# ReLU-squared attention and a SwiGLU block on one core: the second half's norm on VectorE, head groups of four and early second-half scores in batch 0, and stream slots that begin another group

## The chip, the cores and the metric

The kernel runs on one core of a Trainium2 chip. The metric is device time in microseconds of that core. The kernel before took 448.42 us (median of 3 runs, 448.09 to 448.57). The profile is one further execution of the same program; it took 447.78 us, of which the instructions span 446.0 us.

A core has a matrix engine (TensorE, PE in the profile; PEld is its weight loads), VectorE (DVE), ScalarE (ACT), GpSimd (POOL, which here issues nearly all loads) and SyncE (SP, which here issues DMA transposes and the stores). Each engine runs its own instructions in the order in which the program lists them, and waits on semaphores for the others.

## The reference

```python
# q, k, v: (8, 12, 448, 64) float32;  S = 448, D = 64
scores = matmul(q, k.T) / sqrt(D)
attn   = maximum(scores, 0)**2 / S
x      = matmul(attn, v)                 # heads side by side: (3584, 768)

rms = sqrt(mean(x*x, axis=-1) + 1e-6)
xn  = x / rms * rms_g
g   = xn @ w_gate                        # 768 x 1536
val = xn @ w_val                         # 768 x 1536
out = (g * sigmoid(g) * val) @ w_out     # 1536 x 768
```

There is no softmax, so the scores need only a ReLU and a square. The norm needs the sum of squares over all twelve heads of a token; nothing of the feed-forward part of a batch can begin before that batch's attention is complete.

## The kernel before

**Tiling.** There are eight batches of 448 tokens. Scores are made transposed (keys on partitions, queries along the row), two heads of a pair at a time, into a pair of PSUM banks; a rectangle r of 128 x 896 is made by a ReLU (ScalarE, line 459, or VectorE, line 457) and squared in place by VectorE (line 462). `attend` (line 597) multiplies four heads' rectangles with v, ScalarE writes the result as xT (line 632). `rest` (line 511) makes the scores of the last 64 keys of two head pairs. Rectangles live in a ring of 14 SBUF tiles, `r_ring`; a rectangle can be made only when the `attend` that read its tile last is over.

Batch 0 alone is cut into two halves of 224 queries (`halves`, `attention_half(0)` and `attention_half(HS)`, scores on line 493), so that the feed-forward part can begin when half of the queries have been attended. Its q and k are loaded in three pieces of heads (0-2, 2-6, 6-12) and turned on TensorE (`transposes`, lines 412 and 420; VectorE copies the result out, line 430). For each half of batch 0 `Sums` (line 857) adds up the squares over the heads with a matrix of ones, and `norm_scale` makes 1/rms on ScalarE as Exp(-0.5 Ln(mean + eps)) (lines 675 and 679). This needs the Ln/Exp table, and Silu needs another: a table load (line 383) stands on either side. Six VectorE instructions (line 684) then make xn.

**The stream.** The feed-forward part (line 809) is a stream of groups. A group accumulates one output tile in one PSUM bank: a gate or value projection over 6 blocks of 128 contraction rows, or an output projection over 12. Each block is split into its upper and lower 64 rows (half 0 and half 1), which run in different halves of the array. A slot of the stream (`Stream.step`) takes one matmul of half 0 from one group (the lead) and one of half 1 from another (the follow), so that both halves of the array work; where `pick` finds no lead or no follow the slot holds one half only. A group enters with half 0 and ends with half 1. In the quarter form each of these is cut again into two of 64 columns. Silu (line 880), the product with the value (hT, line 894) and the copies of the output (line 954) empty the banks.

**What sets the order.** The whole program is listed by a planner that runs when the kernel is built. Every piece of work is an `Op` with a cost for each engine that can do it, the ops that it needs, a rank and sometimes a due time; `Planner.run` lets time pass by these costs, gives each engine the ready op of the lowest rank, and lists the instructions in that order. The costs are not times of the chip: they decide order alone. A change of a rank or of a dependency therefore moves instructions in the whole program. Where the planner sees TensorE idle for over 0.3 us in the early part, `fill` lists matmuls of zeros (line 1071) that nobody reads.

**Queues.** POOL issues the loads in the order of the `load` calls, each waiting until the eighth load before it has landed (`pool_dma`). They are q, k and v of batch 0, the eight slices of the gate and value weights, q, k, v of batch 1, the output weights, and then the later batches. k of batch 0 is staged in the tile of the output weights, wo_sb.

Of the kernel before, what the change touches and what calls it, by code (L numbers as in the profile page):

```python
# [9 lines left out]
BF16 = mybir.dt.bfloat16  # L10
ALU = mybir.AluOpType
# [8 lines left out]
class Op:  # L20


    def __init__(self, on, fn, deps=(), rank=0, pair=None, bank=False, ends=None, due=None, ring=None,
                 early=0.0, lean=(), form=None):
        self.on, self.ring, self.early = on, ring, early
        self.fn, self.deps, self.rank = fn, list(deps), rank
        self.pair, self.bank, self.ends, self.due = pair, bank, ends, due
        self.done = self.left = NEVER
        self.lean, self.form = dict(lean), form
        self.ps = None  # L30
# [15 lines left out]
class Ring:  # L46


    def __init__(self, tiles):
        self.tiles, self.users, self.at = tiles, [[] for _ in tiles], 0  # L50

    def ready(self):
        return max((u.done for u in self.users[self.at]), default=0.0)
# [1 line left out]
    def take(self, users):  # L55
        n = self.at
        self.before = self.users[n]
        self.users[n], self.at = list(users), (n + 1) % len(self.tiles)
        return self.tiles[n]


class Planner:
# [105 lines left out]
def kernel(  # L168
# [52 lines left out]
    def tiles(n, shape, dtype, name):  # L221
        return [work.tile(shape, dtype, name=f"{name}{i}", tag=f"{name}{i}") for i in range(n)]

    r_ring = Ring(tiles(14, [P, 2, S], BF16, "r"))
    sil_ring = Ring(tiles(3, [P, S], BF16, "sil"))
    ost_ring = Ring(tiles(3, [P, DM], FP32, "ost"))
    xT_of = tiles(2, [P, KT, S], BF16, "xT")
    xn_of = tiles(2, [P, KT, S], BF16, "xn")
    acc_of = tiles(2, [P, 2, S], FP32, "acc")
    x2 = tiles(1, [P, 2, S], FP32, "x2")[0]  # L230
    sum_of = tiles(2, [P, S], BF16, "ssum")
    rstd_of = tiles(2, [P, S], FP32, "rstd")
    hT = tiles(1, [P, FT, 2 * S], BF16, "hT")[0]
# [213 lines left out]

    def evict_rect(t, n, key, group):

        r = r_ring.take([Later(avs, group)])  # L450
        rects[key] = r

        def relu(op):
            op.view = r[:, :, : n // 2]
            src = t.ps.tile[:, :, : n // 2]
            if op.engine == "DVE":
                nc.vector.tensor_relu(out=op.view, in_=src)  # L457
            else:
                nc.scalar.activation(out=op.view, in_=src, func=ACT.Relu)  # L459

        def square(op):
            nc.vector.tensor_tensor(out=rl.view, in0=rl.view, in1=rl.view, op=ALU.mult)  # L462

        rl = add(Op({"ACT": 0.05 + n * 0.833e-3, "DVE": 0.07 + n * 1.042e-3}, relu,
                    [t] + r_ring.before, rank=2, lean={"DVE": 0.5 if key[:2] == (0, 0) else 1.5 if key[0] == 0 else 0.9}))
        sq = add(Op({"DVE": 0.06 + n * 0.53e-3}, square, [rl], rank=3))
        return rl, sq

    def scores_full(b, j, c, due):
# [57 lines left out]
    def rest(b, j, lo, w, due):  # L527
        def fn(op):
            emit_rest(op.ps.tile, b, j, lo, w)
            rl, sq = evict_rect(op, 2 * w, (b, lo, j, "rest"), (b, lo, j))  # L530
            rests[b, lo, j] = (sq, rl)
            plan.take(op.ps.banks, [rl])

        need = [Turned(b, j), Turned(b, j + 1)] + ([Issued(ones[b, lo, j - 2])] if j else [])
        return add(Op({"PE": 0.0025 + w / 2400.0}, fn, need, rank=-4 if j else -1,
                      pair=wide, due=due, form="q", ring=r_ring, early=0.4))

    class Turned(Op):
# [127 lines left out]

    xns, xn_ops = {}, {}

    def norm_scale(b, lo, w, g):

        rstd = accs[b, lo][2]

        def root(op):
            act_set(LN_EXP)
            nc.scalar.activation(
                out=rstd[:, :w], in_=g.ps[:, :w], func=ACT.Ln, scale=1.0 / float(DM),
                bias=eps_col[:],
            )
            nc.scalar.activation(out=rstd[:, :w], in_=rstd[:, :w], func=ACT.Exp, scale=-0.5)  # L679

        def scale(kt):
            def fn(op):
                xns[b] = xn_of[b % 2]
                nc.vector.scalar_tensor_tensor(  # L684
                    out=xns[b][:, kt, lo : lo + w], in0=xTs[b][:, kt, lo : lo + w],
                    scalar=g_sb[:, kt : kt + 1], in1=rstd[:, :w], op0=ALU.mult, op1=ALU.mult,
                )
            return fn

        rt = add(Op({"ACT": lambda: 2 * (0.22 + w * 0.833e-3) + switch(LN_EXP)}, root, [g.end],  # L690
                    rank=-1))
        plan.take(g.space.banks, [rt])
        xn_ops[b, lo] = [
            add(Op({"DVE": 0.126 + w * 1.05e-3}, scale(kt), [rt], rank=-1)) for kt in range(KT)
        ]
        add(Op({"ACT": lambda: switch(SILU)}, lambda op: act_set(SILU), [rt], rank=6))

    def ready_for_norm(b):
        need = [Later(sil, (b, FT - 1, lo)) for lo, _ in halves(b)]
# [3 lines left out]
    class Stream:  # L703
# [38 lines left out]

        def step(self, t):
            lead = self.pick(0, None, t)
            if lead is not None and lead not in self.open:
                self.todo.remove(lead)
                self.open.append(lead)
                lead.begin()
            follow = self.pick(1, lead, t)
            pair = [(half, g) for half, g in ((0, lead), (1, follow)) if g is not None]  # L750
            assert pair
            state["quarters"] = any(g.quarters for _, g in pair) or any(
                g.quarters and g.count[0] for g in self.open
            )
            for m in blocks():
                for half, g in pair:
                    g.emit(half, *m)
            for half, g in pair:
                g.emitted(half, t)
            self.at = [lead, follow]  # L760
            self.steps += 1
            took = max(g.slot for _, g in pair) + plan.changed(form())
            if follow is not None and follow.count[1] == follow.n:
                self.open.remove(follow)
                follow.finish(t)
            note = pair[0][1].note
            if note is not None:
                state["phase"] = note
            return took
# [248 lines left out]
    def now():  # L1018
        return True

    def attention_half(lo):
        for j in range(0, HP, 2):
            if lo == 0:
                transposes(0, j)
                transposes(0, j + 1)
            for jj in range(2):
                scores_half(0, lo, [(j + jj, 0), (j + jj, 1)], now)
            scores_half(0, lo, [(j, 2), (j + 1, 2)], now)
            if j == 0:
                rest(0, 0, lo, HS, now)  # L1030
            attend(0, j, lo, HS, now)
            if j + 2 < HP:
                rest(0, j + 2, lo, HS, now)

    def attention_full(b):
# [38 lines left out]

    load("q", 0, 0, 2)
    load("k", 0, 0, 2)
    load("q", 0, 2, 6)
    load("k", 0, 2, 6)
    made["ident"] = add(Op({"POOL": 0.6}, lambda op: masks.make_identity(nc, ident[:])))
    load("q", 0, 6, 12)  # L1080
    load("k", 0, 6, 12)
    load("v", 0, 0, 6)
    load("v", 0, 6, 12)
    for s in range(NSL):
# [5 lines left out]
    load_wo(0, 2)  # L1090
    load_wo(1, 2)

    attention_half(0)
    first = Sums(0, [(0,), (2,), (4,)])
    for b in range(B):
        groups = ffn(b)
        if b == 0:
# [66 lines left out]
```

## Time and profile before

| what | value |
|---|---|
| median of 3 runs | 448.42 us (448.09 to 448.57) |
| the profiled execution: its time, its span | 447.78 us, 446.0 us |
| PE busy | 440.7 us (99%), 7846 matmuls |
| of these, matmuls of zeros | 110, busy 14.5 us |
| ACT, DVE, POOL busy | 268.2, 240.2, 76.6 us |
| ACT table loads | 18, 23.1 us |
| first slot of the stream begins | 27.24 us |
| first slot with batch 0's second half | 50.4 us |

Busy time of PE counts every matmul, those of zeros as well, and an overlap of matmuls once. "x" is a number of instructions. The chain is the work that ended last, followed backwards, so each of its pieces held up the next.

### The profile page before, as it was taken

How to read it: one execution, taken by the hardware profiler on the slowest of the kernel's cores; microseconds unless marked ns; L12 is line 12 of the kernel's file. 1: busy time of each engine (PE TensorE's matmuls, PEld its weight loads, DVE VectorE, ACT ScalarE, POOL GpSimd, SP SyncE). 2: the span in 40 equal slices, each digit the busy share in tenths (PEclk: the TensorE clock that was granted, in tenths of full speed). 3: DMA queues.
4: the chain of work that ended last, by engine and by line, in shares of the span. 5: the costliest groups of instructions: out<-in, count | busy, mean ns of one | idle time of the engine just before them, and what ended most of it. 6: DMA issues, size and time to landing. Idle time of an engine off the chain costs nothing.

```text
span 446.0 us, 17081 instructions
## 1 busy us (share of the span) xinstructions
PE 440.7 (99%) x7846; PEld 328.6 (74%) x7846; DVE 240.2 (54%) x401; ACT 268.2 (60%) x395; POOL 76.6 (17%) x96
## 2 busy tenths in 40 slices
PE   8999999999999999999999999999999999999996
PEld 7678776877868777678779765678778755687785
DVE  1975786475645455466656347466655446432210
ACT  1677696586648665586757666587657666342212
POOL 8522710070080070070000350010000000000000
PEclk9999999999999999999999999999999999999999
DMA  9999999899899799599005899880002200030004
GB/s 109 196 204 201 202 188 86 137 186 112 99 135 126 139 188 103 107 175 125 1 4 96 153 177 54 114 161 20 3 1 69 75 5 3 1 93 17 3 10 134
DMA packets 130359, 44.75 MB, mean 100 GB/s; under 512 B 102256, under 2 KB 126832, under 8 KB 130288
## 3 DMA queue, kind: packets, MB, share of 16 engines
q0 software_dynamic: 90912, 24.39, 58.5%
q1 hardware_dynamic: 38992, 18.94, 21.3%
q8 instruction: 61, 1.00, 0.9%
q10 hardware_dynamic: 384, 0.34, 0.3%
q14 instruction: 10, 0.08, 0.1%
HBM read 48.76 MB, written 11.01 MB: 134 GB/s over the span
## 4 chain that ended last, share of the span: by engine, by line
PE 97%; DVE 1%; ACT 0%; issue 0%
PE psP L809 78%; PE psS L597 7%; PE psS L475 6%; PE psP L1071 3%; PE psS L511 1%; PE psP L420 1%; PE psS L493 1%; DVE r L462 1%; PE psP L857 0%; PE psP L412 0%; DVE qkT L430 0%; DVE r L457 0%; ACT r L459 0%; DVE xn L636 0%; ACT ost L954 0%
## 5 line engine op out<-in xcount | busy, mean ns | idle before, releaser
L809 PE MATMUL psP<-xn,wg_sb 64*64 64x448 bf16 (+1 forms) x2304 | 219.5, 339 | 0.1
L809 PE MATMUL psP<-xn,wv_sb 64*64 64x448 bf16 (+1 forms) x2304 | 202.8, 339 | 0.2
L459 ACT ACTIVATE r<-psS 128x896 bf16<-128x896 f32 (+1 forms) x168 | 147.7, 913 | 47.8 <-PE psS L475 23.1
L809 PEld LDWEIGHTS <-wg_sb 64*64 64x64 bf16 (+1 forms) x2304 | 122.2, 105 | 36.1 <-PE psP L809 8.0
L462 DVE TENSOR_TENSOR r<-r 128x896 bf16<-128x896 bf16 (+1 forms) x171 | 102.4, 614 | 72.7 <-ACT r L459 72.0
L809 PE MATMUL psP<-wo_sb,hT 64*128 64x384 bf16 (+2 forms) x1526 | 139.4, 321 | 0.0
L809 PEld LDWEIGHTS <-wv_sb 64*64 64x64 bf16 (+1 forms) x2304 | 117.0, 105 | 29.3 <-issue 4.4
L809 PEld LDWEIGHTS <-hT 64*128 64x128 bf16 (+1 forms) x1526 | 102.3, 96 | 22.4 <-issue 2.4
L894 DVE TENSOR_TENSOR hT<-sil,psP 128x448 bf16<-128x448 bf16 (+1 forms) x108 | 60.9, 566 | 64.2 <-PE psP L809 49.9
L880 ACT ACTIVATE sil<-psP 128x448 bf16<-128x448 f32 (+1 forms) x108 | 54.6, 507 | 64.7 <-PE psP L809 55.1
L954 ACT COPY ost<-psP 128x384 f32<-128x384 f32 (+1 forms) x56 | 26.5, 474 | 44.0 <-PE psP L809 42.7
L475 PE MATMUL psS<-qkT 64*64 64x448 bf16 (+1 forms) x412 | 49.8, 350 | 0.0
L597 PE MATMUL psS<-r,vb 64*64 64x448 bf16 (+1 forms) x756 | 46.0, 331 | 0.1
L291 POOL DMA_DIRECT2D vb<-in_v_dram x20 | 14.2, 722 | 179.4 <-PE psS L475 99.9
L684 DVE SCALAR_TENSOR_TENSOR xn<-xT,g_sb,rstd 128x448 bf16<-128x448 bf16 (+1 forms) x54 | 30.3, 629 | 22.7 <-ACT rstd L679 22.7
L307 POOL DMA_DIRECT2D kb<-in_k_dram x42 | 33.3, 1025 | 17.4 <-DMA wo_sb<-in_moe_w_out_dram 9.4
L597 PEld LDWEIGHTS <-vb 64*64 64x64 bf16 x756 | 24.6, 106 | 9.7 <-issue 1.4
L632 ACT ACTIVATE xT<-psS 128x896 bf16<-128x896 f32 (+1 forms) x27 | 22.5, 833 | 14.2 <-PE psS L597 14.1
L475 PEld LDWEIGHTS <-qkT 64*64 64x64 bf16 (+1 forms) x412 | 21.4, 103 | 6.2 <-issue 0.4
L383 ACT ACT_TABLE_LOAD x18 | 23.1, 1283 | 1.0 <-PEq L1148 0.7
L642 DVE TENSOR_TENSOR x<-xT 128x896 f32<-128x896 bf16 x14 | 15.2, 1089 | 6.7 <-ACT xT L632 6.7
L1071 PE MATMUL psP<-busy_bf,ones_bf 128*128 128x224 bf16 x110 | 14.5, 291 | 1.3 <-DVE eps_col L368 1.3
(41 smaller groups left out, 144.1 us busy)
## 6 DMA issues: line engine op xcount, KB each, us to landing
vb<-in_v_dram POOLq DMA_DIRECT2D x12, 384.0 KB, 7.7
qb<-in_q_dram POOLq DMA_DIRECT2D x6, 672.0 KB, 13.8
kb<-in_k_dram POOLq DMA_DIRECT2D x42, 96.0 KB, 12.5
out_dram<-ost SPq DMA_DIRECT2D x7, 336.0 KB, 3.0
wg_sb<-in_moe_w_gate_dram POOLq DMA_DIRECT2D x4, 576.0 KB, 15.9
wv_sb<-in_moe_w_val_dram POOLq DMA_DIRECT2D x4, 576.0 KB, 17.2
wo_sb<-in_moe_w_out_dram POOLq DMA_DIRECT2D x2, 1152.0 KB, 15.1
out_dram<-ost SPq DMA_DIRECT2D x8, 288.0 KB, 4.5
```

The source lines that it names most:

```text
L307: behind_of[b] = nc.gpsimd.dma_start(out=to[:, u - u0 : u - u0 + step, h0:h1, :], in_=rows[:, u : u + step])
L383: nc.scalar.add_instruction(mybir.InstLoadActFuncSet(name=name, act_func_set_id=n, ins=[], outs=[]))
L459: nc.scalar.activation(out=op.view, in_=src, func=ACT.Relu)
L462: nc.vector.tensor_tensor(out=rl.view, in0=rl.view, in1=rl.view, op=ALU.mult)
L475: nc.tensor.matmul(out=ps[m0:m1, hh, :S], lhsT=qkT[b][prt, j, 0, c * P + m0 : c * P + m1], rhs=qkT[b][prt, j, 1, :], start=True, stop=True,)
L597: mm = nc.tensor.matmul(out=ps[hh * D : (hh + 1) * D, jj, :w], lhsT=vb[prt, 2 * (j + jj) + hh, u * D : (u + 1) * D], rhs=r[prt, hh, :], st ...
L684: nc.vector.scalar_tensor_tensor(out=xns[b][:, kt, lo : lo + w], in0=xTs[b][:, kt, lo : lo + w], scalar=g_sb[:, kt : kt + 1], in1=rstd[:, ...
L809: mm = nc.tensor.matmul(out=self.ps[m0:m1, : self.w], lhsT=self.lhsT(i)[prt, m0:m1], rhs=self.rhs(i)[prt], start=(half == 0 and i == 0), s ...
L880: nc.scalar.activation(out=s[:, :w], in_=g.ps[:, :w], func=ACT.Silu)
L894: nc.vector.tensor_tensor(out=hT[:, fb, o : o + w], in0=sil[b, fb, lo][1][:, :w], in1=g.ps[:, :w], op=ALU.mult,)
L954: nc.scalar.copy(out=to, in_=g.ps[:, :w])
L1071: nc.tensor.matmul(out=s.tile[:, :HS], lhsT=ones_bf[:], rhs=busy_bf[:, :HS], start=True, stop=True)
```

## The change

There are four parts.

1. **Loads and order of batch 0.** q and k come in four groups of heads (0-2, 2-4, 4-8, 8-12) in place of three, which makes eight loads of them in place of six. The scores of the second half for the first four head pairs are offered beside those of the first half (`half_scores(HS, j, early)`, which prefers them while the planner's time is under 13), and the `rest` of a head pair no longer waits for the `attend` before it. Evictions of these early scores have a later rank (`aside`). `Sums` of the first half is created ahead of the attention.
2. **More places for rectangles.** Six more tiles, each used once, are views of x2 and of the two acc tiles, which batch 0 does not otherwise use before its norm.
3. **The second half's norm.** `inverse_root` makes 1/rms of batch 0's second half with eleven VectorE instructions of 128 x 224 (a first guess by an integer shift, then two refining steps), in place of Ln and Exp on ScalarE with their two table loads. Their scratch space is x2.
4. **Stream.** Where a slot of batches 1 to 6 has a lead but no follow, and another group could begin, that other group becomes the lead and the first one may serve a later slot.

```diff
 class Ring:
-    def __init__(self, tiles):
-        self.tiles, self.users, self.at = tiles, [[] for _ in tiles], 0
+    def __init__(self, tiles, once=()):
+        self.tiles, self.keep = list(tiles) + list(once), len(tiles)
+        self.users, self.at = [[] for _ in self.tiles], 0
...
-        return self.tiles[n]
+        tile = self.tiles[n]
+        if self.at == 0:
+            del self.tiles[self.keep :]
+        return tile
...
-    r_ring = Ring(tiles(14, [P, 2, S], BF16, "r"))
...
+    spare = []
+    for t in (x2, *acc_of):
+        flat = t.bitcast(BF16)
+        spare += [flat[:, i, :].rearrange("p (t s) -> p t s", t=2) for i in range(2)]
+    r_ring = Ring(tiles(14, [P, 2, S], BF16, "r"), spare)
...
     def evict_rect(t, n, key, group):
+        aside = key[:2] == (0, HS) and not first.end.done < NEVER
...
-                    [t] + r_ring.before, rank=2, lean={"DVE": 0.5 if key[:2] == (0, 0) else 1.5 if key[0] == 0 else 0.9}))
-        sq = add(Op({"DVE": 0.06 + n * 0.53e-3}, square, [rl], rank=3))
+                    [t] + r_ring.before, rank=4 if aside else 2, lean={"DVE": 0.5 if key[:2] == (0, 0) else 1.5 if key[0] == 0 else 0.9}))
+        sq = add(Op({"DVE": 0.06 + n * 0.53e-3}, square, [rl], rank=5 if aside else 3))
...
-        need = [Turned(b, j), Turned(b, j + 1)] + ([Issued(ones[b, lo, j - 2])] if j else [])
+        need = [Turned(b, j), Turned(b, j + 1)] + ([Issued(ones[b, lo, j - 2])] if j and (b or lo) else [])
...
+    def inverse_root(g, y, w):
+        x, h, t = (x2[:, i // 2, i % 2 * HS : i % 2 * HS + w] for i in range(3))
+        as_int = lambda v: v.bitcast(mybir.dt.int32)
+        ts, tt, stt = nc.vector.tensor_scalar, nc.vector.tensor_tensor, nc.vector.scalar_tensor_tensor
+        steps = [
+            lambda: ts(out=x, in0=g.ps[:, :w], scalar1=1.0 / float(DM), scalar2=eps, op0=ALU.mult, op1=ALU.add),
+            lambda: ts(out=as_int(h), in0=as_int(x), scalar1=1, scalar2=None, op0=ALU.logical_shift_right),
+            lambda: ts(out=as_int(y), in0=as_int(h), scalar1=-1.0, scalar2=float(0x5F3759DF), op0=ALU.mult, op1=ALU.add),
+            lambda: tt(out=h, in0=y, in1=y, op=ALU.mult),
+            lambda: tt(out=h, in0=h, in1=x, op=ALU.mult),
+            lambda: ts(out=t, in0=h, scalar1=0.375, scalar2=-1.25, op0=ALU.mult, op1=ALU.add),
...
+            lambda: stt(out=y, in0=t, scalar=1.5, in1=y, op0=ALU.add, op1=ALU.mult),
+        ]
...
-        rt = add(Op({"ACT": lambda: 2 * (0.22 + w * 0.833e-3) + switch(LN_EXP)}, root, [g.end],
-                    rank=-1))
-        plan.take(g.space.banks, [rt])
+        if (b, lo) == (0, HS):
+            rt = inverse_root(g, rstd[:, :w], w)
+        else:
+            rt = add(Op({"ACT": lambda: 2 * (0.22 + w * 0.833e-3) + switch(LN_EXP)}, root, [g.end],
+                        rank=-1))
+            plan.take(g.space.banks, [rt])
...
-        add(Op({"ACT": lambda: switch(SILU)}, lambda op: act_set(SILU), [rt], rank=6))
+        add(Op({"ACT": lambda: switch(SILU)}, lambda op: act_set(SILU), [rt], rank=6 if b else -1))
...
         def step(self, t):
             lead = self.pick(0, None, t)
+            follow = self.pick(1, lead, t)
+            if lead is not None and follow is None and lead.note and 0 < lead.note[0] < B - 1:
+                for g, r in self.options(0, lead):
+                    if g is not lead and lead.last == 0 and r <= t + self.CLOSE:
+                        lead = g
+                        follow = self.pick(1, g, t)
+                        break
...
+    def early():
+        return plan.now < 13.0
+    EARLY = 4
+    def half_scores(lo, j, due):
+        for jj in range(2):
+            scores_half(0, lo, [(j + jj, 0), (j + jj, 1)], due)
+        scores_half(0, lo, [(j, 2), (j + 1, 2)], due)
+        if j == 0 or not lo:
+            rest(0, j, lo, HS, due)
...
+            if lo == 0 or j >= EARLY:
+                half_scores(lo, j, now)
+            if lo == 0 and j < EARLY:
+                half_scores(HS, j, early)
             attend(0, j, lo, HS, now)
-            if j + 2 < HP:
+            if lo and j + 2 < HP:
                 rest(0, j + 2, lo, HS, now)
...
-    load("q", 0, 2, 6)
-    load("k", 0, 2, 6)
+    load("q", 0, 2, 4)
+    load("k", 0, 2, 4)
...
-    load("q", 0, 6, 12)
-    load("k", 0, 6, 12)
+    for h in (4, 8):
+        load("q", 0, h, h + 4)
+        load("k", 0, h, h + 4)
...
+    first = Sums(0, [(0,), (2,), (4,)])
     attention_half(0)
-    first = Sums(0, [(0,), (2,), (4,)])
```

## The prediction

> **What bounds the kernel now.** I read the page first, then the chain in order of time, then the timeline of ScalarE where the chain looked odd, and last the busy time by stretch.
>
> ```profile
> span 446.0 us, 17081 instructions
> PE 440.7 (99%) x7846; PEld 328.6 (74%) x7846; DVE 240.2 (54%) x401; ACT 268.2 (60%) x395; POOL 76.6 (17%) x96
> ...
> L1071 PE MATMUL psP<-busy_bf,ones_bf 128*128 128x224 bf16 x110 | 14.5, 291 | 1.3 <-DVE eps_col L368 1.3
> ```
>
> TensorE is the bound: it is never idle for long, and no other engine passes 60%. But 99% is no proof that nothing can be gained. 110 matmuls are zeros, and a slot of the stream with one half takes as long as a slot with two. So the question is how much of TensorE's time is empty. The chain shows it (start, length, what):
>
> ```profile
> 1.29 6.56 PE psP L1071 x42
> ...
> 9.60 1.06 PE psP L1071 x10
> ...
> 32.49 0.51 PE psS L597 x16
> 32.99 0.10 PE psS L511 x4
> ...
> 33.29 0.41 PE psS L597 x12
> ...
> 33.91 0.20 PE psS L493 x4
> ...
> 45.84 0.97 PE psP L809 x12
> 46.81 0.05 issue
> 46.86 2.78 PE psP L809 x40
> ```
>
> After the first 42, a matmul of zeros takes 1.06/10 = 0.106 us, and there are 68 of them before the stream begins at 27.24. At 45.84, 12 matmuls of the stream take 0.97 us and the next 40 take 2.78; in pairs at 0.095 us a slot (batch 0's slots of 224 start 0.095 to 0.096 apart) they would take 0.57 and 1.90. What is late there, ScalarE's timeline tells:
>
> ```profile
> 43.55 1.28 ACT L383 ACT_TABLE_LOAD   x1
> 44.84 0.45 ACT L675 ACTIVATE rstd<-psP,eps_col 128x224 f32<-128x224 f32 x1
> 45.32 0.39 ACT L679 ACTIVATE rstd<-rstd 128x224 f32<-128x224 f32 x1
> 45.73 1.28 ACT L383 ACT_TABLE_LOAD   x1
> 47.02 0.61 ACT L880 ACTIVATE sil<-psP 128x224 bf16<-128x224 f32 x2
> ```
>
> From 43.55 to 47.02 no Silu runs, so banks of the stream stay full and it finds no second group to pair. The second half's own first slot begins only at 50.42, when its xn (last one ended at 48.0) had long been there: the norm's harm is the blocked ScalarE.
>
> From 60 us on PE is busy 382.5 of 382.6 us; no engine and no DMA makes it wait. There a gain can come only from fewer slots. A stretch late in the kernel, from the chain:
>
> ```profile
> 387.97 8.06 PE psP L809 x93
> ```
>
> 93 matmuls in pairs at 0.1625 us would be 7.56 us. Six of them stand alone (six starts in a row 0.162 apart, from 391.57): (93+6)/2 = 49.5 slots, 8.04 us. A lone half costs a full slot.
>
> **The change part by part.** The order of the two programs, instruction by instruction, gives the counts; the trace of before gives the prices.
>
> *Head (loads in fours, early scores, 20 places for rectangles).* Ahead of the first slot of the stream stand 110 matmuls of zeros before and 86 after; real work moved ahead of it is 5 scores (0.20 each), 2 rests (0.10) and one attend (0.51 + 0.41): 2.1 us. If the first slot begins when it did, TensorE has 2.1 us less behind it; the 24 zeros fewer are 24 x 0.106 = 2.5 us. I take -2.3, with -2.6 and 0 as ends: 0 where the first slot is late by as much.
>
> Is it late? It needs the first half's Ln, which follows ScalarE's evictions. Before, 7 rectangles of 896, 3 of 448 and 3 xT stand ahead of it; after, 14, 4 and 3. Three of 896 in a row take 2.56 us (0.82 apart), the small ones 0.54: 14 x 0.82 + 4 x 0.54 + 3 x 0.55 = 15.3 us of the 16.15 us between the first ReLU (9.64) and Ln (25.79). It fits with 0.8 us left, where before it had 7. At 0.92 each, as a lone one takes, it is 16.7: 0.5 late. I take +0.2 (0 to +0.5).
>
> *Two more loads.* Each costs POOL 0.62 to 0.79 us of issue, so v and the first weight slices are issued up to 1.4 us later. DMA is the limit there: weight slices land 2.9 us apart (23.61, 26.51, 29.47, ... 41.06) in the order of bytes, and POOL sat idle until a landing before four loads between 21 and 30 (1.59, 2.10, 2.13 and 2.30 us). I take 0; without that cover it is +1.4. The order on SP moves two stores of 0.3 to 0.45 us ahead of a block of transposes; after 60 us nothing waits for a DMA on the chain: 0.
>
> *Form switches.* Changes between whole, half-row, quarter and transpose forms rise from 72 to 77. Weight loads show 0.17 to 0.18 us of idle at such a switch, partly under running matmuls; I take 0.12 each, +0.6 (0 to +0.9).
>
> *Second half's norm.* ScalarE loses two table loads, Ln and Exp (3.4 us). The empty part of the chain at 45.8, (0.97 + 2.78) - (0.57 + 1.90) = 1.3 us, and 0.1 of issue, go: -1.4 (-1.0 where some lone slots remain there).
>
> VectorE gains 11 instructions of 128 x 224 on a chain of dependence. No row shows them; the nearest are line 684 (0.38 each in a row of six) and hT of 224 (0.34), and, far off, 1.09 for an fp32 result of four times the size (line 642). At 0.38 they are 4.2 us, with three hT between them (1.1) and six xn (2.3): 7.6 us from the sum to the last xn. In the new order 92 slots of the first half stand between that sum and the first slot of the second half, 92 x 0.095 = 8.8 us. So the root is covered, with 1.2 us left; at 1.09 it would not be, and 6.6 us would lie open. But one product hT is due every 12 slots (1.15 us), and three root steps with one hT take 1.5: hT runs late and a bank comes free late. +0.3 (0 to +1.0).
>
> The Trainium skill, "VectorE: DVE Perf Modes", Mode 2x_2P, has fp32 steps with one tensor from SBUF at two elements a cycle, and those with two tensors at one: as an estimate three steps of 0.12 and eight of 0.23 us, 2.2 us in all before what each instruction costs to start; by that hT would not be late, and the sum would be 0.3 better. No row of before has such steps.
>
> *Stream.* All slots: 2053 before, 2031 after. By length: 12 fewer of 224 (those are the norm's stretch above), 6 fewer of 448, 4 fewer of 384. Slots of 448 start 0.189 apart: 6 x 0.189 + 4 x 0.1625 = -1.8. Some lone slots next to scores already cost only 0.045 to 0.06, so the other end is -1.2. More slots now pair two output pieces in the quarter form (21 against 2). Around the one at 247.64, thirteen starts in a row take 2.37 us, no more than at 0.189 each, so that is free.
>
> Sum: -2.3 + 0.2 + 0.6 - 1.4 + 0.3 - 1.8 = -4.4 us. The profiled execution took 447.78 us (span 446.0 and 1.8 around it): 443.4. The median shown is 0.64 above that execution, so on the median's footing 448.42 - 4.4 = 444.0 us.
>
> **The rivals.**
>
> *ScalarE becomes the bound of the head.* For it: 0.8 us left of 16. Against: an eviction in a row starts every 0.82 us. If the first slot slips by all that was moved, the head's -2.3 goes: 446.3.
>
> *TensorE's clock drops in the head.* For it: the first 42 zeros took 0.156 us each and the later ones 0.106, so there is a slow state at the start, and the change takes out zeros that fill pauses. Against: the longest pause left is filled with zeros too (13 of them). One return as long as the first stretch costs 42 x 0.05 = 2.1 us: 446.1. The Trainium skill, "TensorE: Matmul & The Clock Gate", Part 1, states such a gate: half clock until one window of about 3.4 us has been busy, and again after an idle one. The trace agrees as to the start; by that rule, as an estimate, one window at half clock costs 1.7 us, and the sum would be -2.7.
>
> *The stream's new choice gains nothing*, since starting a group early only moves the lone half elsewhere on the chip: without -1.8 it is 445.8. Against: the count of slots is in the program.
>
> *Slower: banks.* A group that begins earlier holds a bank earlier, and its predecessor must have been emptied. Lone slots of 448 and 384 fall by 21, and each is a place where TensorE could wait for a Silu or a copy. It decides at 4.4/21 = 0.21 us a place. One whole Silu (0.51) at each would be 10.7 - 4.4 = +6.3: 454.7. Against: Silu waits 55.1 us of its 64.7 us of idle for TensorE, hT 49.9 of 64.2: the emptying engines wait for TensorE, not it for them.
>
> **How the numbers follow.** The forecast, with its terms between their ends, 0.80; ScalarE's bound 0.08; the clock 0.04; no gain in the stream 0.03; slower 0.05. The best ends give -2.6 - 1.4 - 1.8 = -5.8, about 442.5. Upwards the range takes in the first three rivals: 446.4. The measurement can tell 0.2%, 0.9 us, from no change. Faster 0.91, same 0.03 (a rival together with bad ends), slower 0.06.
>
> **What would show it.** Right: some 88 matmuls of zeros; the first slot at 27.0 to 27.8 us; ScalarE nearly without idle from 12 to 23; 16 table loads; no lone run near 45; the second half's first slot some 4 us sooner than 50.4; and at 391 us no run of six lone slots. Wrong: a first slot after 29, root steps near 1 us each, or PE idle after 60 us. If the lead over before is large at 60 us and is lost later, the stream did it.

## The result and the profile after

| | before | after |
|---|---|---|
| median of runs | 448.25 us (447.95 to 448.57, 4 runs) | 443.37 us (441.81 to 445.33, 4 runs) |
| the profiled execution: time, span | 447.78 us, 446.0 us | 441.81 us, 440.0 us |

The ratio is 0.989, with a 95% interval of 0.9869 to 0.9912: the change makes the kernel faster by 4.9 us, and 4.4 was forecast. The sum is close, but not for the reasons given. One thing in the table was forecast nowhere: the runs of the kernel after lie 3.5 us apart, those of the kernel before 0.6. (Four runs are few: in the experiments below 20, 17 and 23 further runs of the kernel before lie 2.4, 2.3 and 1.9 us apart.)

The page after, whose lines answer to those shown of before (TensorE, then the table loads):

```profile
span 440.0 us, 17134 instructions
PE 433.7 (99%) x7861; PEld 355.3 (81%) x7861; DVE 242.8 (55%) x414; ACT 264.5 (60%) x389; POOL 77.8 (18%) x98
...
L392 ACT ACT_TABLE_LOAD x16 | 20.5, 1283 | 1.0 <-PEq L1207 0.7
```

TensorE is busy 7.0 us less, with 15 matmuls more. The matmuls of zeros, asked for by their line, are 88:

```profile
L1129 PE MATMUL psP<-busy_bf,ones_bf x88: 259/259/391, 1.3 to 43.9; 128*128 128x224 bf16 x88
```

The chain of waits through the head and the second half's norm (start, length, what):

```profile
1.30 5.84 PE psP L1129 x42
...
16.67 2.97 ACT r L469 x4
19.64 0.44 ACT xT L642
20.08 1.25 ACT x L469 x2
21.33 0.44 ACT xT L642
21.76 2.44 ACT acc L469 x3
...
37.54 6.31 PE psP L856 x116
43.85 0.30 PE psP L1129 x2
44.14 5.61 PE psP L856 x106
```

From 16.67 to 24.20 the chain runs along ScalarE's evictions: the end of the head now is ScalarE's. Behind it the stream runs from 37.54 to 49.75 with little between.

The first 42 matmuls of zeros, the same in both kernels, took 5.84 us here and 6.56 in the profile of before. This start varies from one execution to the next: in the 14 traces of this case the first matmul that is not zeros begins at 6.76 to 8.14 us, whatever the kernel. So 0.7 us of every lead in the next table is chance and not the change's.

The lead over before, taken from the starts of the same piece of work in the two traces:

| first matmul of | before | after | lead |
|---|---|---|---|
| the stream | 27.24 | 27.26 | 0.0 |
| the second half of batch 0 in it | 50.42 | 46.96 | 3.5 |
| batch 1's feed-forward | 90.36 | 87.35 | 3.0 |
| batch 4's feed-forward | 246.45 | 242.65 | 3.8 |
| batch 7's feed-forward | 396.44 | 390.27 | 6.2 |
| end: the last matmul | 442.39 | 436.43 | 6.0 |

So 3 us are won by the start of batch 1's feed-forward, 2.3 of them by the change, where the terms for the head and the norm made 3.2 (2.6 with the form switches). As much again comes behind it, where 1.8 was forecast for the stream. In between the lead is held back: here TensorE stands still, which it did not before. Busy time of TensorE by stretch, after (us in the stretch, us busy):

```profile
27.00:60.00 33.00, 33.00 (x616) 1.00 1.33 203
60.00:430.00 370.00, 368.71 (x6750) 1.00 0.80 88
```

Before, 369.88 of the same 370 were busy. Two stretches of the chain after, at 88 and 207 us, say where:

```profile
87.32 0.43 POOL vb L300
...
88.05 11.67 DMA vb<-in_v_dram
99.72 0.04 issue
99.77 0.94 PE psS L607 x14
...
103.92 0.28 issue
104.20 0.57 PE psP L856 x6
```

```profile
205.75 1.89 PE psP L856 x40
207.64 0.77 issue
208.41 0.57 PE psP L856 x8
```

At 99.77 the `attend` of batch 2 waits for v of that batch. The second of its two loads is issued at 88.05 and lands at 99.72. Before, it was issued at 88.86, landed at 98.29 and was used at 98.77. So the load began 0.8 us sooner, but took 11.7 us in place of 9.4; why is not shown. TensorE comes to this `attend` at 99.08, no sooner than before: its lead of 3 us is taken up by 69 more matmuls of the stream that the new order lists ahead of it. At 103.92 and 207.64 "issue" stands alone: TensorE waits for nothing that the profile shows.

### The profile page after: what moved, and what is told of

The parts are those of the page before. It is cut to its first block, busy times and chain, and to the rows that moved or that the text cites. A ratio compares the mean times of both kernels' runs of the same rounds, so it can differ in the third digit from the quotient of the medians.

```text
span 440.0 us, 17134 instructions
## 1 busy us (share of the span) xinstructions
PE 433.7 (99%) x7861; PEld 355.3 (81%) x7861; DVE 242.8 (55%) x414; ACT 264.5 (60%) x389; POOL 77.8 (18%) x98
## 4 chain that ended last, share of the span: by engine, by line
PE 94%; DMA 3%; ACT 2%; issue 0%; DVE 0%; POOL 0%; POOLq 0%
PE psP L856 76%; PE psS L607 7%; PE psS L485 5%; DMA vb<-in_v_dram 3%; PE psP L1129 2%; PE psP L429 1%; PE psS L521 1%; PE psS L503 1%; ACT r L469 1%; ACT acc L469 1%; PE psP L421 0%; ACT x L469 0%; PE psP L904 0%; ACT xT L642 0%; DVE acc L472 0%
## 5 line engine op out<-in xcount | busy, mean ns | idle before, releaser
L856 PE MATMUL psP<-xn,wg_sb 64*64 64x448 bf16 (+1 forms) x2304 | 234.0, 338 | 0.0
L856 PE MATMUL psP<-xn,wv_sb 64*64 64x448 bf16 (+1 forms) x2304 | 216.9, 338 | 1.0 <-issue 1.0
L469 ACT ACTIVATE r<-psS 128x896 bf16<-128x896 f32 (+1 forms) x164 | 145.4, 919 | 61.1 <-PE psS L485 32.9
L856 PEld LDWEIGHTS <-wg_sb 64*64 64x64 bf16 (+1 forms) x2304 | 134.2, 105 | 18.3 <-issue 3.8
L856 PEld LDWEIGHTS <-wv_sb 64*64 64x64 bf16 (+1 forms) x2304 | 134.3, 105 | 14.8 <-issue 3.4
L472 DVE TENSOR_TENSOR r<-r 128x896 bf16<-128x896 bf16 (+1 forms) x165 | 98.7, 616 | 68.6 <-ACT r L469 67.6
L856 PEld LDWEIGHTS <-hT 64*128 64x128 bf16 (+1 forms) x1563 | 99.8, 97 | 23.9 <-issue 3.5
L1001 ACT COPY ost<-psP 128x384 f32<-128x384 f32 (+1 forms) x52 | 24.5, 471 | 41.0 <-PE psP L856 40.5
L607 PEld LDWEIGHTS <-vb 64*64 64x64 bf16 x756 | 26.6, 106 | 8.6 <-issue 1.6
L654 DVE TENSOR_TENSOR acc<-acc,x 128x896 f32<-128x896 f32 x14 | 15.3, 1092 | 0.5
```

The lines of the kernel that those rows point to most:

```text
L607: mm = nc.tensor.matmul(out=ps[hh * D : (hh + 1) * D, jj, :w], lhsT=vb[prt, 2 * (j + jj) + hh, u * D : (u + 1) * D], rhs=r[prt, hh, :], st ...
L856: mm = nc.tensor.matmul(out=self.ps[m0:m1, : self.w], lhsT=self.lhsT(i)[prt, m0:m1], rhs=self.rhs(i)[prt], start=(half == 0 and i == 0), s ...
L1001: nc.scalar.copy(out=to, in_=g.ps[:, :w])
```

## The experiments

### Is the spread the program's, and what is v of batch 2 worth?

e1 is the changed kernel again, with no edit. e2 issues the load of v for batch 2 ahead of the transposes of its q and k, in place of behind them:

```diff
+            if not b:
+                load("v", b + 2, deps=last)
             load("k", b + 2, deps=seen + [Issued(o) for o in landed["q", b + 2][0]])
             transpose_dma(b + 2, last)
-            load("v", b + 2, deps=turned[b + 2])
+            if b:
+                load("v", b + 2, deps=turned[b + 2])
...
-                if b >= PE_T and not u0:
+                if b > PE_T and not u0:
```

(The second place drops the order that put the load behind the last transpose, for this batch.) Expected of e1:

> The changed kernel, untouched, once more. Its four first runs spread from 441.81 to 445.33 us, where before spread over 0.6 us. Theory A (the arrival of v of batch 2 ends a wait of TensorE, 0.7 us of it in the first trace, and that arrival varies): spread of 2 to 4 us again, median 443 to 444, and a second trace shows a wait for vb at its first use of batch 2 whose length goes with the span. Theory B (short stalls of TensorE in which the profile shows no wait, 0.77 us at 207.64 in the first trace): the second trace has several such stalls at other places, and the wait for vb stays below 1 us. Theory C (the slow clock at the start, 5.84 against 6.56 us for the first 42 matmuls of zeros): the spread is below 1 us, as it would be for before too.

and of e2:

> v of batch 2 is loaded between q and k of batch 2, ahead of the transposes, instead of after them; nothing else of the loads moves. Theory A: the wait at the first use of vb in batch 2 is gone, v has landed before 80 us, the median falls by 0.7 to 2 us against the changed kernel (441.5 to 442.7) and the spread falls below 1.5 us. Theory B: the trace loses the wait at 99.7 but keeps stalls of 0.5 to 1 us without a shown wait, and the spread stays 2 us or more. If the transposes were close to their users, it would get slower; they land at 87 us and are first used after 125, so I expect no cost.

e1 took 443.48 us (442.36 to 445.32, 6 runs), 0.9891 of before (0.9868 to 0.9914): the gain and the spread came back. Its profile shows no wait for v, and four pauses without a shown wait: theory B. The start (theory C) can be a part of the spread at most: it differs by 1.4 us among all traces, and these runs lie 3.0 us apart. e2 took 441.43 us (440.70 to 442.05, 4 runs), 0.9838 of before (0.9818 to 0.9858). It beats both kernels, the changed one by 2 us. The chain of e2 through the place where the kernel after waited:

```profile
102.93 0.76 PE psP L856 x16
103.68 0.76 PE psS L607 x16
```

No wait for v is left, and no "issue". v of batch 2 cost 0.6 us in the profiled execution of the kernel after, so the larger part of the 2 us is something else: pauses without a shown wait, of which e2's profile has one (0.84 us, ending at 207.68), that of the kernel after two and e1's four. Which part of e2's edit removes them is not shown: with v sooner, the loads behind it and TensorE's own order move as well.

### The parts taken back

e3 keeps the loads, the early scores and the places for rectangles alone: the norm's and the stream's parts are undone.

```diff
-        if (b, lo) == (0, HS):
-            rt = inverse_root(g, rstd[:, :w], w)
-        else:
-            rt = add(Op({"ACT": lambda: 2 * (0.22 + w * 0.833e-3) + switch(LN_EXP)}, root, [g.end],
-                        rank=-1))
+        rt = add(Op({"ACT": lambda: 2 * (0.22 + w * 0.833e-3) + switch(LN_EXP)}, root, [g.end],
+                    rank=-1))
...
-            if lead is not None and follow is None and lead.note and 0 < lead.note[0] < B - 1:
-                for g, r in self.options(0, lead):
...
```

(The Silu table's load behind the norm also gets its old rank back here; e8 below leaves it at the new one.)

> Loads in fours, early scores and the 20 places alone; the norm on ScalarE and the stream as before. By my steps: 24 zeros fewer and 2.1 us of work moved ahead (-2.3), first slot 0.2 late, switches +0.6, and 5 slots fewer: 445.7 to 446.9, i.e. -1.5 to -2.7 against before. Rival (ScalarE bounds the head, nothing gained): 448 to 448.6, with the first slot 2 us later than 27.24.

It took 445.88 us (444.83 to 448.00, 9 runs), 0.9943 of before (0.9925 to 0.9962): 2.6 us, within the 1.5 to 2.7 expected.

e4 undoes the choice in the stream alone (the last lines of the diff above).

> The changed kernel with the stream's old choice of the lead. 2040 slots against 2031: 8 more lone halves of 448 and 10 more of 384. By my steps +1.5 us against the changed kernel (1.2 to 1.8): 444.9 if that is at 443.4. Rival (the new choice moves lone halves elsewhere and gains nothing): within 0.3 us of the changed kernel.

It took 447.87 us (445.57 to 451.65, 12 runs), 0.9988 of before (0.9965 to 1.0011). The stream's part, forecast at 1.8, is worth 4.4 between these medians, far more than its 9 slots of 0.16 to 0.19 us. So either slots are not the measure, or the pauses hide something; its runs lie 6 us apart.

### What the pauses are

In all these traces I counted TensorE's instructions in the order of their starts (weight loads, matmuls, and the 22 of its sequencer that the trace shows), and noted the number of the instruction behind each pause of over 0.45 us after 60 us (the end of the program left out; length from one start to the next):

```
kernel   pause ends   length   instruction   number modulo 256
after        99.77      0.59      3360           32   (waits for v of batch 2)
            104.21      0.63      3521          193
            208.41      1.12      7361          193
e1           98.08      0.67      3265          193
            105.37      1.23      3521          193
            173.69      0.91      6081          193
            209.44      0.54      7361          193
e2          207.68      0.84      7361          193
e3          172.92      0.82      6081          193
            204.48      1.69      7105          193
e4           97.89      0.90      3265          193
            105.18      1.23      3521          193
before        none
```

All pauses but the one known wait come once in 256 instructions, at the same place in the count. The queue table of the page has a queue that moves such blocks:

```profile
q0 software_dynamic: 90944, 24.39, 62.1%
...
q8 instruction: 61, 1.00, 1.0%
```

61 packets of 16384 bytes, one for each 256 of TensorE's 15,722 weight loads and matmuls. In the trace the last such packet before a pause starts 2.2 to 3.4 us before the pause ends and lands 1.2 to 1.7 us before. Where the DMA engines are quiet the packet starts right behind the boundary before, a whole block (6 us) ahead of need; under the loads, in the cases listed, 150 to 220 of the 256 instructions have gone before it starts. The theory: these are instruction fetches that the loads delay. Two experiments test it.

e5 to e8 leave out all loads and transposes of batches 3 to 7. TensorE's order of instructions is not changed by it.

```diff
             def whole(prt=prt, n=n, u0=u0, u1=u1):
+                if b > 2:
+                    ld[nm, b] = ld[nm, b - 2]
+                    return
...
                 def piece(prt=prt, n=n, u=u, u0=u0, step=step):
+                    if b > 2:
+                        return
...
             def turn(op, nm=nm, c=c):
+                if b > 2:
+                    qkT[b] = qkT[b - 2]
+                    return
```

e5 is the changed kernel with this edit, e6 the kernel before with it:

> The changed kernel without the loads and transposes of batches 3 to 7 (they use q, k and v of the batch two before, so the output of these batches is another); TensorE's instructions and their order are those of the changed kernel. Theory F (the pauses of TensorE that no wait explains are late instruction fetches, delayed by the loads' traffic): no such pause after 105 us, runs within 0.5 us of each other, and the profiled 441.81 less its pauses of 0.63 and 1.12 us: 440.1 to 440.6. Rival N (the pauses have nothing to do with the loads): pauses of 0.5 us and more remain behind 105 us, and the time stays at 443.4 with runs 3 us apart.

> The kernel before without the loads and transposes of batches 3 to 7 (they use q, k and v of the batch two before, so the output of these batches is another). Theory F: the profiled execution of before had no such pause and took 447.78, so 447.4 to 447.9, runs within 0.5 us; the change is then worth 7.0 to 7.6 us where neither kernel is disturbed. Rival N: 448.3, and the change is worth 5 as in the first comparison.

e5 took 441.19 us (440.02 to 444.31, 6 runs, five of them within 440.02 to 441.45), e6 447.45 us (446.86 to 447.99, 11 runs). The theory's 440.1 to 440.6 for e5 was 0.6 too low, and one run of six stands apart; but after 105 us no pause is left. TensorE's busy time in the stretch, of e5:

```profile
105.00:430.00 325.00, 325.00 (x6024) 1.00 0.11 30
```

and of the kernel after:

```profile
105.00:430.00 325.00, 324.23 (x6004) 1.00 0.69 80
```

The one pause that e5 keeps (0.93 us, ending at 98.16, instruction 3265, 193 modulo 256) lies under the loads of batch 2, which it still has. Removing the loads is worth 0.9 us to the kernel before and 2.2 to the changed one. Why the same loads cost the changed program more is not shown.

e9 tests the place. The first 42 matmuls of zeros are made 84 of half the width, so that every later instruction has a number 84 higher:

```diff
-        for _ in range(int((t1 - t0 - 0.15) / 0.1)):
-            nc.tensor.matmul(out=s.tile[:, :HS], lhsT=ones_bf[:], rhs=busy_bf[:, :HS], start=True, stop=True)
+        n = 1 if t0 > 5.0 else 2
+        for _ in range(n * int((t1 - t0 - 0.15) / 0.1)):
+            nc.tensor.matmul(out=s.tile[:, : HS // n], lhsT=ones_bf[:], rhs=busy_bf[:, : HS // n], start=True, stop=True)
```

> The changed kernel whose first 42 matmuls of zeros are 84 of half the width: the same time, but every later instruction of TensorE has a number that is 84 higher. Theory F (late instruction fetches): pauses of 0.5 us and more that no wait explains come at the same numbers as before, 193 more than a multiple of 256, and so at work that stands 84 instructions earlier in the program. Rival (a wait at that piece of work): they come at the same work, at numbers 21 more than a multiple of 256. Time by both 443.4, in the changed kernel's range of 441.8 to 445.3.

```
pause ends   length   instruction   number modulo 256
  101.09      1.61      3444          116   (3360 + 84: waits for v of batch 2)
  110.00      1.07      3777          193
  178.35      0.95      6337          193
  202.69      1.28      7105          193
  209.71      1.10      7361          193
```

The wait for v moved with its work; the four others stayed with the number. (For the one at 110.00 the chain also shows a Silu that ended at 109.74.) The time was 445.27 us (442.85 to 445.82, 6 runs), 1.9 over the forecast, though the ranges overlap: ten runs of the changed kernel, with e1, have a median of 443.5 and reach 445.33. The profiled execution was e9's slowest and that of the changed kernel its fastest; of the 4.0 us between these two, the five pauses here and the three there account for 3.7. So where the boundaries fall can be worth up to 2 us in this kernel, as far as six runs tell, and a change of a few instructions in the head can move that. The chain of e9 around two of them:

```profile
200.28 1.48 PE psP L856 x30
201.76 0.93 issue
202.70 1.13 PE psP L856 x18
...
208.94 0.02 PE psS L485 x2
208.96 0.76 issue
209.71 0.38 PE psS L485 x2
```

At 208.96 the pause splits the four matmuls of one score in the middle, though the last two read the same tile as the first two.

The Trainium skill, "Runtime: NRT & Kernel Launch", Instruction fetch mechanics, says that instructions come in blocks of 256 over a queue of the sequencer's own, and that crossing into the next block is mostly hidden. The trace agrees on the block. That it is hidden holds here while few loads run (e5 after 105 us, no pause); under the loads a crossing cost up to 1.7 us.

### What the stream's part is worth without pauses

e7 is the changed kernel with the old choice in the stream, e8 the one with Ln and Exp on ScalarE again (the first part of e3's diff), both without the later loads.

> The changed kernel with the old choice in the stream, without the loads and transposes of batches 3 to 7 (they use q, k and v of the batch two before). 9 more slots than the changed kernel. Theory S1 (the choice is worth its slots, 9 times 0.16 to 0.19, and the rest of the 4.4 us measured between the medians was late fetches): 1.5 to 1.7 over the changed kernel's undisturbed run, 441.7 to 442.3. Theory S2 (a lone half costs more than a slot, and the choice is worth about 4): 444.1 to 444.8.

> The changed kernel with Ln and Exp on ScalarE for the second half's norm, without the loads and transposes of batches 3 to 7 (they use q, k and v of the batch two before). By the prediction's terms (-1.4 for the lone slots near 45 us, +0.3 for a late hT) 1.1 over the changed kernel's undisturbed run: 441.2 to 441.7. By its 8 more slots and 2 fewer zeros, at 0.095 to 0.189: 0.6 to 1.3 over. Rival: the blocked ScalarE lies beside other work in the new order, and nothing is lost: 440.1 to 440.6.

e7 took 444.77 us (444.47 to 445.21, 4 runs): the choice is worth 3.6 us, with e5's one pause counted against it. Theory S1, slots alone, falls. e8 took 441.53 us (440.79 to 442.42, 4 runs), 0.3 over e5 between medians, where 1.1 was forecast. The medians do not settle it: e5's profile has the pause of 0.93 us that e8's has not, and counted from the stream's first slot to the last matmul, without what that pause adds (0.74: its 0.93 less a slot), e5's execution is 1.2 us the shorter.

Where do 3.6 us come from, if 13 slots fewer after 60 us are 1.95? I added up what the slots take from 60 us on, and set against it what they would take at 0.189 (448 columns), 0.1625 (384), 0.095 (224) and 0.083 us (192) each (light: without the later loads):

```
kernel             slots after 60 us   take     at those rates   over
e6  before, light        1852         327.2        320.8          6.4
e12 stream only, light   1844         323.4        319.4          4.0
e10 handover, light      1879         327.4        324.5          2.8
e7  stream undone, light 1806         322.2        316.3          5.9
e5  after, light         1793         318.6        314.4          4.2  (0.7 of it the one pause)
```

Slots are longer than they should be, and more so in the old order. The chain of before shows it regularly; of the kernel before:

```profile
257.30 2.33 PE psP L809 x48
259.63 0.38 PE psS L475 x8
260.00 2.33 PE psP L809 x48
```

and of the kernel after:

```profile
255.74 2.27 PE psP L856 x48
258.01 0.19 PE psS L485 x4
258.19 2.27 PE psP L856 x48
```

48 matmuls of 64 x 64 are 12 slots, 2.27 us at 0.189. Before, 0.06 is lost in each dozen. In the trace of e7 two slots in a row take 0.227 and 0.213 there, just where a group's lower half begins one slot after its upper half has ended. The program makes the lower half wait for the last matmul of the upper one (an empty instruction in `Group.emit` carries the wait); with one slot between, that matmul is not over. In the order of the program, handovers with exactly one slot and no other work between are 104 before, 61 in the changed kernel and 95 in the changed one with the old choice. (A narrower count stands behind the 85 and 43 in the expectation below and the 30 in e12's.) Those with 448 columns in the quarter form, 40 in e6, take some 0.037 us over their time in the mean; with two slots between, nothing is lost.

To price the handover by itself, e10 changes only the distance that the planner reckons with, in the kernel before:

```diff
-            t = self.when + max(self.slot, 0.2) if self.last not in (None, half) else 0.0
+            t = self.when + max(self.slot, 0.25) if self.last not in (None, half) else 0.0
```

> The kernel before, in which the planner reckons 0.25 us and not 0.2 from the last upper half of a group to its first lower half, so that at least two slots lie between; without the loads and transposes of batches 3 to 7 (they use q, k and v of the batch two before). 20 slots more (7 of 224, 3 of 384, 10 of 448: 3.0 us), and next to no group that is handed over with one slot between, where there were 85, 43 of them with 448 columns in the quarter form at 0.037 us over their time. Theory H (the handover is the cost of these): 447.45 + 3.0 - 1.6 = 448.9. Rival (slots count alone): 450.5.

It took 447.18 us (446.47 to 447.63, 11 runs), 0.3 less than e6 and 1.7 less than even theory H allowed, though it has 20 slots more: 27 more after 60 us, 3.7 us at the rates above, against which the waits inside slots fall by 3.6, twice what I had put on the 43 handovers that I had priced; 85 at 0.037 would be 3.1. Its chain has the full rate:

```profile
253.66 2.27 PE psP L817 x48
255.93 0.19 PE psS L483 x4
256.12 2.27 PE psP L817 x48
```

So a slot that is saved is worth nothing by itself if it brings groups nearer to their own upper halves. That all of the 3.6 are handovers is not shown; the list above says only that they went when the distance grew.

### The norm and the stream alone

e11 is the kernel before with part 3 alone, e12 with part 4 alone (both as in the change's diff, and without the later loads).

> The kernel before with the second half's norm on VectorE alone, without the loads and transposes of batches 3 to 7 (they use q, k and v of the batch two before). 2 slots more than before (3 of 384 more, 1 of 224 fewer). Theory 1 (the norm's gain needs the early scores; alone the lone slots only move): 447.4 to 448.0. Theory 2 (the prediction's terms, -1.4 and +0.3, hold alone): 446.2 to 446.6.

> The kernel before with the new choice in the stream alone, without the loads and transposes of batches 3 to 7 (they use q, k and v of the batch two before). 8 slots fewer (5 of 384, 3 of 448: 1.4 us) and 30 fewer handovers with one slot between. Theory S1 (slots alone): 446.0. Theory S2 (as undoing it showed, about 0.4 us for each slot saved): 444.0 to 444.6.

e11 took 448.22 us (447.74 to 449.16, 11 runs), 0.8 more than e6 and 0.2 above the range of theory 1: alone the norm on VectorE is a loss. Its profile (449.16 us, the slowest of the eleven) shows where: from 44.69 to 49.78 the chain runs along VectorE, whose eleven steps and four hT between them take 5.4 us, and from the stream's first slot to batch 1's feed-forward it needs 64.6 us where e6 needs 63.1. Of the 30 lone slots of e6 near 45 us some 26 are left, strewn from 48.96 to 59: without the early scores the norm's time is not covered. e12 took 443.73 us (443.49 to 444.01, 4 runs), 3.7 less than e6, of which 1.4 are slots and 2.4 the waits inside them (6.4 to 4.0 in the table): theory S2, and 0.3 below its range.

## Why the prediction was nearly right, point by point

Without the later loads, the change is worth 441.19 - 447.45 = -6.3 us (e5 against e6). Taking single parts back gives -3.6 for the stream (e7) and -0.3 for the norm (e8). What remains, -2.3, I put down to the head; it holds what the parts do together as well, and shrinks by as much as the norm's part is larger than its medians say. The later loads take 2.2 us from the changed kernel and 0.9 from the one before (443.37 - 441.19 and 448.39 - 447.45), which is 1.2 against the change: -6.3 + 1.2 is about -5.0, and 4.9 were measured. By parts, forecast against measured:

| | forecast | measured |
|---|---|---|
| head (-2.3, +0.2), form switches (+0.6) | -1.5 | -2.3 (the remainder) |
| second half's norm (-1.4, +0.3) | -1.1 | -0.3 (by traces up to -1.2) |
| stream | -1.8 | -3.6 |
| transfers | 0 | +1.2 |
| sum | -4.4 | -5.0 |

- *Head, -2.3 with +0.2 for a late start.* The whole came out near its size; the late start was mis-sized, and it is luck that 27.26 lies in the forecast 27.0 to 27.8: the first stretch of zeros took 0.72 us less than in the profile of before. From the first matmul that is not zeros to the first slot it is 19.45 or 19.46 us in all five traces with the old head, and 20.19 to 20.51 in the nine with the new one: 0.7 to 1.1 us late, where +0.2 (0 to +0.5) stood in the sum. The evictions themselves were priced well: from ScalarE's first ReLU to Ln it is 14.9 us, for the 15.3 reckoned. But they were taken to begin when they did before, and they begin 1.8 us later (10.69 - 7.07 against 9.64 - 7.79, both from the first matmul that is not zeros); so the 0.8 us of slack was not there. To this extent the first rival had it right: ScalarE, idle for 0.7 us between 12 and 23, holds up the stream, and the chain runs along it for 7.5 us. What made the gain all the same is the work moved ahead: from the first slot to batch 1's feed-forward it is 60.1 us for the 63.1 before, 0.4 of it the norm's (60.5 in e8). The +0.6 of form switches no run has apart.
- *Two more loads, and the DMAs after 60 us: 0.* Wrong for the second. "After 60 us nothing waits for a DMA on the chain" was read off the kernel before, where v of batch 2 landed 0.48 us ahead of its use. This row showed how little slack there was, and no term was set against it: with a transfer that took 2.3 us longer, TensorE waited 0.6 us in the profiled execution. The fetches of instructions, too, are transfers, and before they came in time: there no pause of 0.45 us stands behind 60 us. "PE idle after 60 us" was named as a sign of being wrong, and it came, 1.3 us in the 370 from 60 to 430.
- *Second half's norm, -1.4 and +0.3 for a late hT.* The costs of the steps were right, the worth was not. On VectorE the eleven steps take 0.28 to 0.39 us, 3.9 in all where 4.2 stood in the sum, and from first to last 4.8 with three hT between, where 5.3 was forecast:

```profile
37.58 0.39 DVE L686 TENSOR_SCALAR x<-psP 128x224 f32<-128x224 f32 x1 [0.64 <-PE psP L904]
38.00 0.28 DVE L687 TENSOR_SCALAR x<-x 128x224 int32<-128x224 int32 x1
...
38.62 0.39 DVE L689 TENSOR_TENSOR x<-rstd 128x224 f32<-128x224 f32 x1
38.93 0.38 DVE L941 TENSOR_TENSOR hT<-sil,psP 128x224 bf16<-128x224 bf16 x1
...
42.44 2.27 DVE L721 SCALAR_TENSOR_TENSOR xn<-xT,g_sb,rstd 128x224 bf16<-128x224 bf16 x6
44.63 0.68 DVE L941 TENSOR_TENSOR hT<-sil,psP 128x224 bf16<-128x224 bf16 x2
```

  But "no lone run near 45" was wrong. Two runs of eight lone slots stand at 42.92 and 44.08, with two zeros between: the six xn in a row hold up hT from 42.44 to 44.63, as ScalarE's table loads held up Silu before. I had hT late by the root's steps, not by the xn behind them. The blocked engine changed, and half of the lone slots stayed (16 for the 30 before). In all it is -0.3 by the medians for the forecast -1.1, by the traces between 0.3 and 1.2, and alone, in e11, a loss.
- The Trainium skill, "VectorE: DVE Perf Modes", Mode 2×_2P, has fp32 steps with one tensor from SBUF at double rate; by that the estimate was 0.12 against 0.23 us. The trace agrees with the difference (0.28 against 0.39), and shows what lay on top of each instruction: 0.16 us.
- *Stream, -1.8.* The sign and the count of slots were right, the price of a slot was not the whole of it: -3.6 without the later loads. The term counted slots at 0.189 and took paired slots to be full. The chain of before held the contradiction (2.33 us for 48 matmuls that should take 2.27). The step "a lone half costs a full slot" was no error, but the new choice also lets the upper halves run farther ahead, and handovers of one slot fall from 95 to 61.
- *Slower by banks:* no sign of it. *The clock:* 1.00 in the stretches after 27 us; the first zeros ran no worse. *The stream gains nothing:* the opposite.
- Of the signs named, "if the lead over before is large at 60 us and is lost later, the stream did it" was a wrong reading: the lead was held back after 90 us, and the transfers did it.

So the sum came out 0.6 from the forecast because what was too low (1.8 in the stream, 0.8 in the head) and what was too high (0.8 in the norm, 1.2 for the transfers) nearly cancel. That they do is luck.

## What to carry to other kernels

Before a bound engine's work is moved ahead, list what it takes from transfers (loads, instruction blocks) with the slack of each: what had half a microsecond left is the next wait. A load that is issued behind something it doesn't need may go ahead of it, as in e2, which is 2 us faster, though the wait for that load was 0.6 of it at most. Compare two traces from the first real work on, not from the span's start: here the start alone differed by 0.7 us and hid a head that had become later. A count of slots is a price only if the slots are full: compare a regular piece of the chain with its count times its rate before using either. And where two versions differ by a microsecond or two in a program of many instructions, look at where the pauses fall: they may belong to the instruction's number and not to the work.

## What the runs showed of the hardware

- TensorE's instructions arrive in blocks of 256 over a DMA queue, and the loads' traffic delays them. Under the loads, 11 pauses of 0.5 to 1.7 us in five profiled executions (after, e1 to e4), all at 193 modulo 256; none after 105 us without the later loads. Filler instructions of zeros count too.
- In the quarter form with 448 columns, a lower half that the program makes wait for an upper half with one slot between costs some 0.04 to 0.06 us; with two slots between, nothing.
- A VectorE step of 128 x 224 in fp32 takes 0.28 us with one tensor from SBUF and 0.39 with two, or with one from PSUM.
- The first 42 matmuls of zeros take 5.84 to 6.56 us in the two profiles compared, the later ones some 0.11 us each; in all 14 traces the first matmul behind them begins at 6.76 to 8.14 us.
